# Cached attention beside a small expert: the first key units in other pieces

## The chip, the core and the metric

The kernel runs on one core of a Trainium2 chip. The metric is device time in microseconds. Before the change three runs took 1275.46, 1275.97 and 1275.99 us; the median is 1275.97. The profile shows one further execution of the same program, which took 1275.56 us.

## What is computed

One token passes a layer norm, and then two branches run side by side, whose results are added to it: attention with grouped queries over a long cache, and a one-token expert.

```
xn = layernorm(x)                       # x: 1 x 448
q  = (xn @ wq)                          # 16 query heads of 256
k, v: 8 heads, 65536 positions of 256, bf16; two query heads share one
p  = softmax(q k^T / 16);  o = p v
out = x + o @ wo + xn + sigmoid(xn @ w_r) * ((silu(xn @ w_gate) * (xn @ w_up)) @ w_down)
```

Keys and values are 537 MB of the 549 MB that the kernel reads. All of it is read once and used for a single token.

## The kernel before

The cache is cut into 32 key units and 32 value units of 8,192 KB (four of each per head): 128 partitions with 128 cache rows of 256 elements each, 64 KB in a partition. The SBUF ring has three slots of one unit. Key units use slots 0 and 1 in turn, value units slot 2. The query weights lie in slot 2 before the first value unit does.

A key unit is worked through in 8 sets of 16 rows per partition. For each set TensorE transposes the keys in 16 matmuls (`ps_t`), VectorE and ScalarE copy the result to `kt_all`, and 8 matmuls form the scores (`ps_q`). Four sets are half a unit. A value unit is one block of 64 matmuls (`ps_o`) with the softmax weights `p_sb`.

TensorE's program is a loop over turns, one for each key unit `u` (`turn_K`, line 790). In turns 0 to 3 there are only keys, since the first head's softmax needs the maximum over its four units. From turn 4 on, the value block of unit `u - 4` stands between the first four sets and the last four. In turn 4 the maximum of head 0 is completed on the way through the first four sets, and the exponentials of head 0 stand before the value block.

Two turns make one pass of TensorE's loop, an even and an odd one, so the waits of all even turns share one place in the code. A wait whose count changes from turn to turn compares with a register there.

SP issues all large transfers on one queue, in a fixed order (lines 306 to 331): two pieces of the query weights, key units 0 to 3, value unit 0, key units 4 and 5, and then value unit and key unit in turn. Each issue waits for the slot to be free: `FREE u` is the last transpose of key unit `u`, `FREEH u` the last of its first half, `VFREE t` the end of value block `t`. SP works these waits off one after the other, so a transfer whose wait isn't met holds back all later ones.

`slot_item` (line 277) issues a unit whole or in pieces; each piece has a semaphore of its own. `HALVED` (line 71) names the key units that are loaded in two halves: 0 to 4. For these SP waits with the first half of unit `u` only for `FREEH u - 2`, and TensorE starts on a unit when its first half has landed (`k_sets`, line 770).

Of the kernel before, what the change touches and what calls it, by code (L numbers as in the profile page):

```python
# [12 lines left out]
CH = 64  # L13
# [11 lines left out]
def bass_parallel_sum__gqa_block_cached__moe_arch_mod__decode_kernel(  # L25
# [36 lines left out]
    SETN = NG * GN  # L62
    CSETS = CH // SETN
    SBN = HC * CH
    SETS = SBN // SETN
    U = NPP // SBN
    NT = U * (Hkv - 1)
    NU = U * Hkv
    NTB = NG
    UH = U + 1  # L70
    HALVED = (0, 1, 2, 3, 4)
    assert rep == 2 and NH == 2 and U * SBN == NPP and U % 2 == 0
    assert 2 * D % P == 0 and RP % 2 == 1 and FK % 2 == 0 and Hq % 2 == 0 and FB <= 512
    inv_sqrt_dh = float(Dh) ** -0.5
# [7 lines left out]
    WQN, WGN, WDN, WON = RP * HqDh // 2, RP * F, FH * D, rep * NH * D  # L82
# [17 lines left out]
    wq_area = slots[2][:, 0:WQN]  # L100
# [100 lines left out]
    def SEM(name):  # L201
        s = nc.semaphore("sem_" + name)
        handles.append(s)
        sems[name] = s.__enter__()
        return name

    for n_ in ["pe", "act", "dve", "pool", "qk", "jt", "evq", "exp", "pc", "qc", "sc", "w0", "out", "wq", "wg", "wo", "wd", "we0", "we1", "we2", "wo2", "wo3", "half0", "half1", "res"]:
        SEM(n_)
    for i in range(NTB):
        SEM(f"ev{i}")  # L210
# [21 lines left out]
    def W(e, *key):  # L232
        put(e, "w", key, None, None)
# [3 lines left out]
    def O(e, key, fn, sem=None, n=1):  # L237
        key = key if isinstance(key, tuple) else (key,)
        if not ghost[0]:
            weight[key] = n  # L240
        put(e, "o", key, fn, sem or e)

    def alias(e, *key, sem=None):
        put(e, "a", key, None, sem or e)
# [14 lines left out]
    items = {}  # L259
# [4 lines left out]
    def item(key, parts, need=()):  # L264
        for n in need:
            W("sp", *n)
        for ap, src, sem in parts:
            semtot[sem] = semtot.get(sem, 0) + 16
            items[key] = (sem, semtot[sem])
            prog["sp"].append(("d", here[0], ("DMA", key, len(prog["sp"])), (ap, src), sem))  # L270

    def rows_src(kd, u, o, J):
        src = A_k_cache if kd == "k" else A_v_cache
        n0 = (u % U) * SBN + o
        return src[0, u // U].rearrange("(p n) d -> p n d", p=P)[:, n0:n0 + J, :]

    def slot_item(kd, u, s, parts=None, need=()):

        o = 0
        for k, (sem, J) in enumerate(parts or [("slot%d" % s, SBN)]):  # L280
            ap = slots[s][:, o * Dh:(o + J) * Dh]
            item((kd, u, k), [(ap.rearrange("p (j d) -> p j d", d=Dh), rows_src(kd, u, o, J), sem)],
                 need[k] if isinstance(need, dict) else need if k == 0 else ())
            o += J
        fed[(kd, u)] = (s, parts or [("slot%d" % s, SBN)])

    def flat_src(src, n):
        return src.rearrange("a b -> (a b)").rearrange("(p n) -> p n", p=P)
# [7 lines left out]
    def k_item(u):  # L296
        need = [("FREE", u - 2)] if u >= 2 else ()
        if u >= 2 and u in HALVED:
            need = {0: [("FREEH", u - 2)], 1: need}
        slot_item("k", u, u % 2, [("slot%d" % (u % 2), CH), ("half%d" % (u % 2), CH)] if u in HALVED else None, need)  # L300

    def v_item(t):
        slot_item("v", t, 2, None, [("VFREE", t - 1)] if t else [("QT",), ("R",), ("CONST",)])

    WQ1 = WQN // 4
    item("wq", [(wq_area[:, a:b], flat_src(A_wq, WQN)[:, a:b], "wq") for a, b in ((0, WQ1), (WQ1, WQN))])
    for u in range(U):
        k_item(u)
    v_item(0)
    k_item(U)  # L310
    k_item(U + 1)
    for t in range(1, NT):
        v_item(t)
# [24 lines left out]
    def W_item(e, key):  # L338
        W(e, "DMA", key)
# [98 lines left out]
    pe = nc.tensor  # L438

    def mm(*a, **k):  # L440
        return pe.matmul(*a, **k)  # L441

    def pe_setup():
        W("pe", "XE")
        W("pe", "CONST")

        def xnt(it):
            for c in range(2 * NE):
                ins = mm(ps_m[0:P, C_XNT + c:C_XNT + c + 1],
                         lhsT=xe_row[0:1, :, :, :].rearrange("o b c p -> o (b c) p")[:, c, :],  # L450
                         rhs=sel_bf[0:1, 0, 0:1], start=True, stop=True)
            return ins

        O("pe", "XNT", xnt, n=16 * U)
        W("pe", "XNTSB")
        W_item("pe", "wq")

        def qrow(it):
            for h in range(RP):
                for j in range(NG):  # L460
                    ins = mm(q_rows[32 * j:32 * j + rep, :], lhsT=xnT_sb[:, 2 * h:2 * h + 2], rhs=wq_area[:, (NG * h + j) * QN:(NG * h + j + 1) * QN],
                             start=h == 0, stop=h == RP - 1, tile_position=(0, 32 * j))
            return ins

        W("pe", "PSQ_ZERO")
        O("pe", "QROW", qrow, "jt", 2)
        W("pe", "QROWSB")

        def qt(it):
            half = Hq * NH // 2  # L470
            for f in range(half // NG):
                w = q_row[0:QROWS, f // NH * Dh:(f // NH + 1) * Dh].rearrange("s (x f) -> s x f", f=NH)[:, :, f % NH]
                ins = mm(ps_m[0:P, C_Q:C_Q + 2 * half].rearrange("p (i j f) -> p j i f", i=rep, j=NG)[:, :, :, f], lhsT=w,
                         rhs=sel_bf[0:QROWS, :, :], start=True, stop=True)
            return ins

        O("pe", "QT", qt, "qk", 2)
        W("pe", "PSO_ZERO")
        W("pe", "S2Z")
        W("pe", "KZ")  # L480
        W("pe", "z_q")
# [5 lines left out]
    def k_T(s, m, ap, j):  # L487
        e = ev_engine(m)
        kv = ap.bitcast(FP32).rearrange("p (j d) -> p j d", d=P)
        W("pe", "EV", s - 1, m)  # L490

        def f(it):
            for jj in range(GN):
                ins = mm(ps_tf[m][:, jj * P:(jj + 1) * P], lhsT=kv[:, j + GN * m + jj, :], rhs=ident_f[:, :],
                         is_transpose=True, start=True, stop=True)
            return ins

        O("pe", ("T", s, m), f, f"t{m}")
        kt, tb = kt_buf[(s * NG + m) % NKT], ps_t[m]
        W(e, "T", s, m)  # L500
        if TORD.index(m) < 2:
            W(e, "QK", s - 1)
        if e == "dve":
            O(e, ("EV", s, m), lambda it: nc.vector.tensor_copy(out=kt[:, :], in_=tb[:, :]), f"ev{m}")  # L504
        else:
            O(e, ("EV", s, m), lambda it: nc.scalar.activation(out=kt[:, :], in_=tb[:, :], func=ACTF.Copy), f"ev{m}")  # L506

    def k_QK(s):
        u, sl = divmod(s, SETS)
        x = sl  # L510
        if x == 0:
            W("pe", "EVQ", u - 1)
        if sl == 0:
            W("pe", "QC", u)
        for m in range(NG):
            W("pe", "EV", s, m)

        def f(it):
            for hf in range(NH):
                for m in range(NG):  # L520
                    kt = kt_buf[(s * NG + m) % NKT]
                    ins = mm(ps_q[32 * m:32 * m + SETS * rep, 0:512], lhsT=q_pad[:, hf, (SETS - 1 - x) * rep:(2 * SETS - 1 - x) * rep],
                             rhs=kt[:, :].rearrange("p (k f) -> p f k", f=NH)[:, hf, :],
                             start=(hf == 0 and x == 0), stop=(hf == NH - 1 and x == SETS - 1), tile_position=(0, 32 * m), skip_group_check=True)
            return ins

        O("pe", ("QK", s), f, "qk")
        if x < SETS - 1:
            return
        W("act", "QK", s)  # L530
        W("act", "JT", u - 2)
        O("act", ("EVQ", u), lambda it: nc.scalar.activation(out=s2[u % 2][0:SROWS, :], in_=ps_q[0:SROWS, :], func=ACTF.Copy), "evq")  # L532
        if sl == SETS - 1 and u < NU - 1:
            O("act", ("QC", u + 1), lambda it: nc.scalar.activation(
                out=q_cur[:, :, :], in_=qT_sb[:, :, bass.ds(it * rep + rep, rep) if u + 1 >= U else slice(0, rep)], func=ACTF.Copy), "qc")
# [234 lines left out]
    def k_sets(u, sets, at):  # L770
        ap = slots[u % 2]
        for q in sets:
            if q % CSETS == 0:
                W_item("pe", ("k", u, 0) if q == 0 else ("k", min(u, UH - 1 - (UH - 1 - u) % 2), 1))
            s = u * SETS + q
            for n, m in enumerate(TORD):
                k_T(s, m, ap, q * SETN)
                if n == NG - 1 and (q + 1) % CSETS == 0:
                    alias("pe", "FREE" if q == SETS - 1 else "FREEH", u, sem=f"t{m}")
                if (q, n) in at:  # L780
                    at[(q, n)]()
                if n == 1:
                    k_QK(s - 1)
            k_JT(s - 2)
# [155 lines left out]
    dve_setup()  # L940
    act_setup()
    pe_setup()
    for u in range(NU):
        turn_K(u)
# [274 lines left out]
```

## Time and profile before

| what | value |
|---|---|
| median of three runs | 1275.97 us |
| profiled execution | 1275.56 us |
| its span | 1274.2 us |
| TensorE (PE) busy | 939.5 us, 74% |
| VectorE (DVE) busy | 571.6 us, 45% |
| ScalarE (ACT) busy | 329.3 us, 26% |
| transfers | 549.18 MB, mean 431 GB/s |

The span runs from the first to the last instruction of the profiled execution; what lies around it is 1.4 us. All times in the rows below are microseconds from the start of the span. Busy shares are means over the whole run, in which several stages follow each other. SPq is the sequencer that issues the transfers.

### The profile page before, as it was taken

The numbers are of one execution on the slowest core, as the hardware profiler recorded it, in microseconds if no ns is written. First come the engines' busy times: TensorE is split into PE (matmuls) and PEld (weight loads), VectorE is DVE, ScalarE is ACT, GpSimd is POOL, SyncE is SP. The second block draws the span as 40 slices with busy tenths as digits, with TensorE's granted clock in tenths as the row PEclk, the third lists the DMA queues.
The fourth block names the chain that finished last, engine by engine and source line by source line (L and its number), as shares of the span: only waits on it lengthen the run. The fifth ranks groups of instructions, "written<-read, shape, count | busy, mean of one in ns | idle before, by whom it ended". The sixth has DMA issues, their size and how long they took to land.

```text
span 1274.2 us, 21262 instructions
## 1 busy us (share of the span) xinstructions
PE 939.5 (74%) x8812; PEld 577.8 (45%) x8812; DVE 571.6 (45%) x1086; ACT 329.3 (26%) x432; POOL 9.1 (1%) x38
## 2 busy tenths in 40 slices
PE   4997977678777679777778776687676687766744
PEld 2665544445444445444445444454344454444412
DVE  5775644355344454443454444454444543434410
ACT  1333422132222322222222222222222222222200
POOL 2000000000000000000000000000000000000000
PEclk9998988789888898888898888898888988888885
DMA  9999999999999999999999999999999999999998
GB/s 405 429 435 426 451 430 430 432 432 434 442 430 430 432 432 436 440 430 430 432 432 440 436 432 428 432 432 440 436 432 428 434 430 446 432 430 428 431 437 364
DMA packets 11812, 549.18 MB, mean 431 GB/s; under 512 B 1303, under 2 KB 1690, under 8 KB 2202
## 3 DMA queue, kind: packets, MB, share of 16 engines
q1 hardware_dynamic: 11796, 549.03, 99.7%
q8 instruction: 7, 0.11, 0.0%
q14 instruction: 3, 0.02, 0.0%
q10 hardware_dynamic: 6, 0.00, 0.0%
HBM read 549.03 MB, written 0.00 MB: 431 GB/s over the span
## 4 chain that ended last, share of the span: by engine, by line
DMA 78%; PE 20%; issue 1%; DVE 0%; ACT 0%; SPq 0%; DVEq 0%
DMA ring<-in_A_v_cache_dram 74%; PE ps_o L441 13%; DMA ring<-in_A_k_cache_dram 5%; PE ps_t L441 5%; PE ps_q L441 1%; PE ps_m L441 1%; PE ps_s L441 0%; DVE kt_all L504 0%; ACT S_sb L590 0%; SPq L983 0%; DVE m1p L560 0%; DVE S_sb L558 0%; ACT p_sb L600 0%; DVE kt_all L932 0%; DVE diag L575 0%
## 5 line engine op out<-in xcount | busy, mean ns | idle before, releaser
L441 PE MATMUL ps_t<-ident_f,ring 128*128 128x128 f32 x4096 | 583.8, 288 | 76.8 <-DMA ring<-in_A_k_cache_dram 76.4
L504 DVE COPY kt_all<-ps_t 128x1024 bf16<-128x1024 bf16 x768 | 489.8, 684 | 293.2 <-PE ps_q L441 287.5
L441 PEld LDWEIGHTS ps_t<-ident_f,ring 128*128 128x128 f32 x4096 | 454.2, 144 | 251.5 <-issue 133.8
L506 ACT ACTIVATE kt_all<-ps_t 128x1024 bf16<-128x1024 bf16 x256 | 261.9, 1023 | 490.1 <-PE ps_t L441 489.8
L441 PE MATMUL ps_o<-ring,p_sb 128*4 128x512 bf16 x2048 | 183.1, 522 | 217.8 <-DMA ring<-in_A_v_cache_dram 214.7
L441 PEld LDWEIGHTS ps_o<-ring,p_sb 128*4 128x4 bf16 x2048 | 54.7, 103 | 313.5 <-issue 292.3
L441 PE MATMUL ps_q<-kt_all,q_pad 128*16 128x512 bf16 x2056 | 168.0, 402 | 4.7 <-DVE kt_all L504 1.3
L613 DVE RECIPROCAL rs<-ps_m 128x4 f32<-128x4 f32 x29 | 5.3, 183 | 277.3 <-PE ps_m L441 277.3
L600 ACT ACTIVATE p_sb<-S_sb 128x128 bf16<-128x128 bf16 x64 | 18.9, 307 | 274.7 <-PE ps_o L441 274.4
L648 DVE CAST ob_sb<-ps_o 100x512 bf16<-100x512 f32 x29 | 20.1, 692 | 101.3 <-PE ps_o L441 101.3
L441 PEld LDWEIGHTS ps_q<-kt_all,q_pad 128*16 128x16 bf16 x2056 | 28.8, 86 | 51.7 <-issue 26.7
L532 ACT ACTIVATE s<-ps_q 112x512 bf16<-112x512 f32 x33 | 19.7, 597 | 118.3 <-PE ps_q L441 118.3
L441 PEld LDWEIGHTS ps_m<-rowsum,ones_f 128*128 128x128 f32 x58 | 12.3, 264 | 23.1 <-issue 23.1
L590 ACT ACTIVATE S_sb<-S_sb,negmax 128x512 bf16<-128x512 bf16 x16 | 13.3, 856 | 23.3 <-DVE negmax L584 23.3
L441 PE MATMUL ps_m<-diag,ones_f 2*128 2x2 f32 x58 | 11.1, 258 | 11.2 <-DVE diag L575 11.2
L441 PEld LDWEIGHTS ps_m<-diag,ones_f 2*128 2x128 f32 x58 | 8.6, 184 | 18.1 <-DVE diag L575 18.1
L560 DVE TENSOR_REDUCE m1p<-S_sb (+1 forms) x33 | 13.9, 422 | 4.4
L441 PE MATMUL ps_m<-rowsum,ones_f 128*128 128x4 f32 x58 | 14.9, 326 | 0.0
L558 DVE CAST S_sb<-ps_s 128x256 f32 (+1 forms) x33 | 13.7, 414 | 1.9 <-PE ps_s L441 1.9
L441 PE MATMUL ps_m<-sel_bf,ring 1*128 1x1 bf16 (+1 forms) x12 | 0.6, 168 | 13.6 <-DVE ring L406 12.8
L441 PE MATMUL ps_s<-sel_bf,s 128*128 128x64 bf16 x132 | 9.2, 193 | 0.7 <-ACT s L532 0.7
L532 ACT ACT_TABLE_LOAD x7 | 9.0, 1283 | 1.3 <-issue 1.2
(97 smaller groups left out, 132.4 us busy)
## 6 DMA issues: line engine op xcount, KB each, us to landing
ring<-in_A_k_cache_dram SPq DMA_DIRECT2D x10, 4096.0 KB, 28.6
ring<-in_A_v_cache_dram SPq DMA_DIRECT2D x2, 4096.0 KB, 27.9
ring<-in_A_wq_dram SPq DMA_DIRECT2D x1, 2688.0 KB, 11.1
ring<-in_B_w_gate_dram SPq DMA_DIRECT2D x1, 1568.0 KB, 16.4
ring<-in_B_w_up_dram SPq DMA_DIRECT2D x1, 1568.0 KB, 19.8
ring<-in_B_w_down_dram SPq DMA_DIRECT2D x1, 1568.0 KB
ring<-in_A_wo_dram SPq DMA_DIRECT2D x1, 1344.0 KB, 35.2
ring<-in_A_wo_dram SPq DMA_DIRECT2D x1, 1120.0 KB, 24.9
```

The source lines that it names most:

```text
L441: return pe.matmul(*a, **k)
L504: O(e, ("EV", s, m), lambda it: nc.vector.tensor_copy(out=kt[:, :], in_=tb[:, :]), f"ev{m}")
L506: O(e, ("EV", s, m), lambda it: nc.scalar.activation(out=kt[:, :], in_=tb[:, :], func=ACTF.Copy), f"ev{m}")
L532: O("act", ("EVQ", u), lambda it: nc.scalar.activation(out=s2[u % 2][0:SROWS, :], in_=ps_q[0:SROWS, :], func=ACTF.Copy), "evq")
L558: O("dve", ("SCOPY", u), lambda it: nc.vector.tensor_copy(out=S_sb[:, at(it, SBN), :], in_=ps_sn), "sc")
L560: O("dve", ("SMAX", u), lambda it: nc.vector.tensor_reduce(out=m1p[:, :, at(it, 1)], in_=S_sb[:, at(it, SBN), :].rearrange("p n i -> p i n ...
L590: O("act", ("EXP", h, i), lambda it, i=i: nc.scalar.activation(out=S_sb[:, :, i], in_=S_sb[:, :, i], func=ACTF.Exp, bias=negmax[:, i:i + 1 ...
L600: O("act", ("PC", t, c), lambda it: nc.scalar.activation(out=p_sb[:, c, :, :], in_=S_sb[:, n:n + CH, :], func=ACTF.Copy), "pc")
L613: O("dve", ("RS", t), lambda it: nc.vector.reciprocal(out=rs[:, :, :], in_=ps_m[0:P, C_TOT:C_TOT + NH * rep]))
L648: O("dve", ("OB", t), lambda it: nc.vector.tensor_copy(out=ob_sb[0:OROWS, :], in_=ps_o[0:OROWS, :]))
```

## The change

Units 1, 2 and 4 are loaded whole, with one semaphore. Unit 3 stays in halves. Unit 0 comes in three pieces: a quarter, a quarter and a half, counted by the semaphores `slot0`, `part` and `half0`. The first piece of the query weights counts on `half1` instead of `wq`; unit 1's wait for a second half, which stands at the same place as unit 3's in the odd turns, is met by that count.

```diff
-    UH = U + 1
-    HALVED = (0, 1, 2, 3, 4)
+    HALVED = (3,)
+    FIRST = (CH // 2, CH // 2, CH)
@@ k_item
-        slot_item("k", u, u % 2, [("slot%d" % (u % 2), CH), ("half%d" % (u % 2), CH)] if u in HALVED else None, need)
+        parts = [("slot%d" % (u % 2), CH), ("half%d" % (u % 2), CH)] if u in HALVED else None
+        slot_item("k", u, u % 2, parts if u else list(zip(("slot0", "part", "half0"), FIRST)), need)
@@ query weights
-    item("wq", [(wq_area[:, a:b], flat_src(A_wq, WQN)[:, a:b], "wq") for a, b in ((0, WQ1), (WQ1, WQN))])
+    for k, (a, b, sem) in enumerate(((0, WQ1, "half1"), (WQ1, WQN, "wq"))):
+        item(("wq", k), [(wq_area[:, a:b], flat_src(A_wq, WQN)[:, a:b], sem)])
+    items[("k", 1, 1)] = items[("wq", 0)]
@@ pe_setup
-        W_item("pe", "wq")
+        W_item("pe", ("wq", 0))
+        W_item("pe", ("wq", 1))
@@ k_sets
-            if q % CSETS == 0:
-                W_item("pe", ("k", u, 0) if q == 0 else ("k", min(u, UH - 1 - (UH - 1 - u) % 2), 1))
+            if q == 0:
+                W_item("pe", ("k", u, 0))
+            elif u % 2 == 0 and q * SETN in (FIRST[0], FIRST[0] + FIRST[1]):
+                W_item("pe", ("k", 0, 1 if q * SETN == FIRST[0] else 2))
+            elif u % 2 and q == CSETS:
+                W_item("pe", ("k", min(u, HALVED[-1]), 1))
```

What stands on SP's queue at the start of the program, before the change (a shape of 128x16384 is half a unit, 128x32768 a whole one; `sem_t2` counts transposes, that is `FREE` and `FREEH`; `sem_pe` counts value blocks, `VFREE`):

```order
L983 DMA ring<-in_A_wq_dram 128x3584
L983 DMA ring<-in_A_wq_dram 128x10752
L983 DMA ring<-in_A_k_cache_dram 128x16384 x4
L983 DMA ring<-in_A_k_cache_dram 128x16384 [waits sem_t2] x4
L983 DMA ring<-in_A_v_cache_dram 128x32768 [waits sem_pool,sem_dve,sem_qk]
L983 DMA ring<-in_A_k_cache_dram 128x16384 [waits sem_t2] x2
L983 DMA ring<-in_A_k_cache_dram 128x32768 [waits sem_t2]
L983 DMA ring<-in_A_v_cache_dram 128x32768 [waits sem_pe]
```

The same place on SP's queue after the change:

```order
L991 DMA ring<-in_A_wq_dram 128x3584
L991 DMA ring<-in_A_wq_dram 128x10752
L991 DMA ring<-in_A_k_cache_dram 128x8192 x2
L991 DMA ring<-in_A_k_cache_dram 128x16384
L991 DMA ring<-in_A_k_cache_dram 128x32768
L991 DMA ring<-in_A_k_cache_dram 128x32768 [waits sem_t2]
L991 DMA ring<-in_A_k_cache_dram 128x16384 [waits sem_t2] x2
L991 DMA ring<-in_A_v_cache_dram 128x32768 [waits sem_pool,sem_dve,sem_qk]
L991 DMA ring<-in_A_k_cache_dram 128x32768 [waits sem_t2] x2
L991 DMA ring<-in_A_v_cache_dram 128x32768 [waits sem_pe]
```

Unit 2 is one transfer behind one wait instead of two behind two. Unit 4 is one transfer as well, and stands with unit 5 after value unit 0. The order of the units is what it was.

TensorE, the first two to three sets of an even turn, before (`ps_s` are the transposed scores of the unit before, `sem_ev0` and the like count the copies out of `ps_t`):

```order
L441 MATMUL ps_s<-sel_bf,s_1 128x32x2 [waits sem_sc]
L441 MATMUL ps_s<-sel_bf,s_1 128x32x2 x3
L441 MATMUL ps_t<-ident_f,ring 128x128 [waits sem_ev0]
L441 MATMUL ps_t<-ident_f,ring 128x128 x3
L441 MATMUL ps_t<-ident_f,ring 128x128 [waits sem_ev1]
```

And after:

```order
L444 MATMUL ps_s<-sel_bf,s_1 128x32x2 [waits sem_sc]
L444 MATMUL ps_s<-sel_bf,s_1 128x32x2 x3
L444 MATMUL ps_t<-ident_f,ring 128x128 [waits sem_ev0,sem_part]
L444 MATMUL ps_t<-ident_f,ring 128x128 x3
L444 MATMUL ps_t<-ident_f,ring 128x128 [waits sem_ev1]
```

The third set of an even turn waits for `part`, which only unit 0 raises; from then on the wait is met. No instruction of TensorE's matmuls has moved.

## Rows read from the trace of the kernel before

**Rows 1.** The page's slices, sums of transfers and the large queue.

```profile
DMA  9999999999999999999999999999999999999998
...
DMA packets 11812, 549.18 MB, mean 431 GB/s; under 512 B 1303, under 2 KB 1690, under 8 KB 2202
...
q1 hardware_dynamic: 11796, 549.03, 99.7%
```

**Rows 2.** What SP's queue waited for: us in total, times, longest.

```profile
SPq L983 <- PE ps_o L441: 798.8, 29, 28.7
```

**Rows 3.** Stretches: length, busy us of PE to POOL, granted clock, DMA share, GB/s.

```profile
2.50:20.00 17.50, 3.80 (x40) 1.25 (x40) 10.21 (x24) 2.07 (x4) 5.96 (x20) 1.00 1.03 440
20.00:112.50 92.50, 88.93 (x784) 60.08 (x784) 63.01 (x107) 34.81 (x40) 0.00 (x0) 1.00 1.00 430
112.50:120.00 7.50, 0.00 (x0) 0.00 (x0) 0.75 (x2) 1.68 (x2) 0.00 (x0) 0.68 0.99 425
...
175.00:1180.00 1005.00, 747.37 (x6974) 462.89 (x6976) 451.30 (x858) 261.88 (x341) 0.00 (x0) 0.89 1.00 434
```

**Rows 4.** The chain that ended last: start, us, what.

```profile
0.81 0.39 SPq L983
...
1.26 0.42 SPq L983
...
1.73 20.31 DMA ring<-in_A_k_cache_dram
...
79.63 40.50 DMA ring<-in_A_k_cache_dram
...
140.15 28.39 DMA ring<-in_A_v_cache_dram
...
168.67 3.58 PE ps_o L441 x32
...
174.92 32.32 DMA ring<-in_A_v_cache_dram
```

**Rows 5.** SP's issues in order of time: start, us, what.

```profile
35.02 0.33 SPq L983 DMA_DIRECT2D ring<-in_A_k_cache_dram  x1
...
46.35 0.33 SPq L983 DMA_DIRECT2D ring<-in_A_k_cache_dram  x1
...
68.46 0.33 SPq L983 DMA_DIRECT2D ring<-in_A_k_cache_dram  x1
...
90.39 0.33 SPq L983 DMA_DIRECT2D ring<-in_A_k_cache_dram  x1
...
112.31 0.33 SPq L983 DMA_DIRECT2D ring<-in_A_k_cache_dram  x1
...
150.82 0.33 SPq L983 DMA_DIRECT2D ring<-in_A_k_cache_dram  x1
...
1272.92 0.26 SPq L983 DMA_DIRECT2D out_dram<-kt_all  x1
```

**Rows 6.** PE in order of time; in brackets the idle time before.

```profile
17.68 0.28 PE L441 MATMUL ps_m<-sel_bf,ring 98*128 98x8 bf16 x4 [0.80 <-DVE ring L429]
22.08 1.97 PE L441 MATMUL ps_t<-ident_f,ring 128*128 128x128 f32 x8 [4.13 <-DMA ring<-in_A_k_cache_dram]
...
120.17 1.97 PE L441 MATMUL ps_t<-ident_f,ring 128*128 128x128 f32 x8 [7.89 <-DMA ring<-in_A_k_cache_dram]
```

**Rows 7.** Half-microsecond stretches, columns as in rows 3.

```profile
114.50:115.00 0.50, 0.00 (x0) 0.00 (x0) 0.00 (x0) 0.50 (x1) 0.00 (x0) 1.00 0.46 197
...
125.00:125.50 0.50, 0.50 (x4) 0.50 (x4) 0.47 (x1) 0.20 (x1) 0.00 (x0) 0.50 1.67 721
125.50:126.00 0.50, 0.50 (x6) 0.44 (x4) 0.23 (x1) 0.00 (x0) 0.00 (x0) 1.00 0.61 262
...
173.00:173.50 0.50, 0.50 (x12) 0.23 (x8) 0.00 (x0) 0.00 (x0) 0.00 (x0) 0.71 2.12 918
```

**Rows 8.** Issues by line: size and us from issue to landing.

```profile
ring<-in_A_wq_dram SPq DMA_DIRECT2D x1, 2688.0 KB, 11.1
```

More of the change, by code (lines that the diff above doesn't have):

```diff
@@ L205, in SEM @@
         return name
-    for n_ in ["pe", "act", "dve", "pool", "qk", "jt", "evq", "exp", "pc", "qc", "sc", "w0", "out", "wq", "wg", "wo", "wd", "we0", "we1", "we2", "wo2", "wo3", "half0", "half1", "res"]:
+    for n_ in ["pe", "act", "dve", "pool", "qk", "jt", "evq", "exp", "pc", "qc", "sc", "w0", "out", "wq", "wg", "wo", "wd", "we0", "we1", "we2", "wo2", "wo3", "half0", "half1", "part", "res"]:
         SEM(n_)
```

## The prediction, on record before the changed kernel ran

> **What bounds the kernel now.** I read the page's slices first: the DMA line stands at 9 in every slice but the last, and one queue's packets fill 99.7% of 16 engines' span [rows 1]. By stretches the DMA share is 0.99 to 1.03 from 2.5 us on, while PE is busy 88.93 of 92.50 us in the stretch 20 to 112.5 and idle in 112.5 to 120 [rows 3]. So the transfers set the time, and whatever PE does, all 549 MB have to come through. A transfer is added to the end only where the queue runs dry. For that the reader needs SP's waits: SP issues each transfer when PE has freed the slot, and it waits a total of 798.8 us for PE's value products [rows 2]. Those waits are harmless as long as the next issue comes before the transfer in flight is done.
>
> The pace comes from the chain of waits. Value landings are 140.15 + 28.39 = 168.54 and 174.92 + 32.32 = 207.24 [rows 4]. Between the two lie one key unit and one value unit: 38.70 us, so 19.35 us for a whole unit. Counted back from 168.54, key unit 5 lands at 149.19, unit 4 at 129.84, v0 at 110.5, unit 3 at 91.1, unit 2 at 71.8, unit 1 at 52.4. Counted forward from the first half of unit 0 (1.73 + 20.31 = 22.04) unit 1 would land at 51.1, so these early landings are known to about 1 us.
>
> **Part by part.** *Query weights under two semaphores, register arithmetic in the even turn gone.* PE waits for both pieces before the same product as before; the one ALU instruction was a sequencer step beside 90 us of PE work. I cost both at nothing; the DMA queue, full at that time, hides them.
>
> *Unit 0 in three.* PE begins at 22.08, when the first half has landed; its setup ends at 17.68 + 0.28 = 17.96 [rows 6]. A quarter lands some 4.8 us earlier than a half (a quarter of 19.35), at 17.2, so PE begins at 18.0. The first half of a unit's sets takes 35.02 − 22.08 = 12.94 us after this start [rows 5, 6], to 30.9; the second half of the unit lands at 31.7 to 32.5, PE takes another 46.35 − 35.02 = 11.33 us [rows 5], and frees slot 0 at about 43.2 instead of 46.35. This 3 us lead is worth nothing: PE waits for unit 1 next.
>
> *Unit 1 whole.* Before, PE went on to unit 1's first half without a stop. Now it waits from 43.2 for the whole unit, at about 52: 9 us idle. It then starts with the clock down, as at 22.08, where the whole unit took 46.35 − 22.08 = 24.3 us; the later units take 90.39 − 68.46 = 21.9 and 112.31 − 90.39 = 21.9 [rows 5]. So units 1, 2 and 3 are freed at 76.3, 98.2 and 120.1, 8 us later than before.
>
> Is any transfer late by that? The rule I use: an issue must come 2.5 us before the preceding transfer lands (that value is worked out below). Unit 2: issue 43.2, limit 49.9. Unit 3, first half: 52 + 12.9 = 64.9, limit 69.3. Unit 3, second half: 76.3, limit 81.4 − 2.5 = 78.9, a margin of 2.6. v0, next in SP's order: right behind it. Unit 4, now whole and so issued at 98.2 instead of 79.63 [rows 4]: limit 108. Unit 5: 120.1, limit 127.3. All are in time.
>
> *Unit 4 whole.* This is the term that counts. In the turn of unit 4 PE does half of its key sets, then the first value block, and the end of that block is what SP waits for to issue v1. Before, the first half landed at 79.63 + 40.50 = 120.13 and v1 was issued at 140.15 [rows 4]: 20.02 us. PE could start half a transfer early. Now it waits for the whole unit: 129.84, less what the three undivided units save. That saving is bounded above by the halved stretch: from 22.04 to 120.13 are 98.09 us for five units, 1.34 more than 5 × 19.35, or 0.27 a unit, 0.8 for three; from below it is 0 (unit 0 has one cut more). I take 0.1: landing at 129.7. PE's work from there is the same list of instructions after an idle time of 9.6 us instead of 7.89 [rows 6], so v1 is issued at 129.7 + 20.0 = 149.7. Its limit is 149.1 − 2.5 = 146.6. It is late, the queue runs dry, and nothing later gives the time back.
>
> The clock is a part of these 20 us. It was granted at 1.00 (2.4 GHz) until after PE stopped, was at 0.50 (1.2 GHz) when PE restarted at 120.17, and came back at 125.5, after 5.3 us of work; after the restart at 168.67 it came back between 173.0 and 173.5, after 4.3 to 4.8 us [rows 4, 6, 7]. Both idle times are long enough for it to fall, so I carry the penalty over unchanged and allow 0.7 us either way, the scatter of such returns.
>
> *The price of an empty queue.* The trace shows only one start into an empty queue with a load of many rows: the query weights, issued at 0.81 and 1.26, the second piece landing 11.1 us after its issue, at 12.36 [rows 4, 8]. Both pieces, a quarter and three quarters of 3,584 KB, are 8.47 us at 19.35 us for 8,192 KB, so from the first issue to the landing 3.1 us lie beyond the transfer. From the other side the tiny output transfer, issued at 1272.92, has landed by the end of the span, 1274.2: 1.3 us at most [rows 5]. I take 2.5, nearer to the weights, which are the same kind of load but have shorter rows. Then v1 lands at 149.7 + 2.5 + 19.35 = 171.55, 3.0 us after 168.54. By the ends: 1.8 and 3.6.
>
> The Trainium skill has a price for this too ("DMA: Bandwidth & Descriptors", section "Anatomy of one DMA — SWDGE (gpsimd) path"): a fit of about 2.0 us fixed plus the bytes over 436 GB/s, measured on another issue path than SP's. By it v1 would take 21.2 us, the loss would be 2.4 us and the time 1278.4. For queued transfers the trace disagrees with paying the fixed part each time, since 38.70 us for two units leave 0.1 us apiece over the fit's variable part [rows 4].
>
> *After v1.* Unit 6 is issued 150.82 − 140.15 = 10.7 us after v1 [rows 4, 5], at 160.4, limit 169. v2 needs the block of turn 5: half a unit of sets after 160.4 brings it to about 177.7 (174.92 before [rows 4]), limit 188. The margin of 10 us is back, and the rest of the run is the old one, shifted. *The end* follows the last landing in both.
>
> **Sum.** The profiled execution took 1275.56 us (span 1274.2). 1275.56 + 3.0 = 1278.56. It lies 0.41 under the median of the runs, 1275.97, so on the scale of the median I forecast 1279.0. A difference of 0.2%, about what a measurement of this kernel can tell from no change, is 2.55 us.
>
> **Rivals.**
> 1. *The late issue is hidden or nearly so.* If PE's 20.0 us shrank by 1 us or more (clock back sooner, unit 4 landing 0.8 sooner) and the restart cost the 1.3 of the lower bound, the loss would be 1275.97 + 0 to 1.5: 1276 to 1277.5. For it: the lateness is only 3 us of a path of 150. Against: the same instructions ran after the same kind of idle time, and all these must come together.
> 2. *A second dry spot before unit 3's second half.* Its margin is 2.6 us, on landings known to 1 us. If unit 1 took 4 us longer than I say (its start with the clock down lasting longer), about 1.5 us would be lost there, and unit 4 and v1 would move by as much: 1280.5. Against: 24.3 us already holds one restart.
> 3. *Faster: the early start of PE is paid out.* The chain of waits runs through PE from 22.08 to 79.63, before it goes over to the transfers [rows 4, 6]. Were the keys' work the limit there, beginning at 18.0 would give back 4.1 us: 1271.9. It would need the queue to have run dry in this stretch, and its share is 1.00 at 430 GB/s against 434 later [rows 3]; the difference, 0.9 us in 92.5, is the most that could be won, and only with v1 in time.
>
> **Chances.** A dry queue before v1 with a loss of 1.5 to 4.3 us: 0.76; of this 0.55 lies over 2.55. Rival 1: 0.13. Rival 2: 0.08. Rival 3 or a small gain of whole pieces: 0.03. So faster 0.03, within 0.2% 0.34, slower 0.63. The range: from 3.0 downward 1.2 for the cheap restart, 0.7 for the clock and 0.5 for the landing of unit 4 give 0.6; upward 0.6, 0.7 and a little of rival 2 give 4.6: 1276.6 to 1280.6.
>
> **What would show it.** PE's first key transposes at about 18.0, and a wait of PE for the key transfer of some 9 us ending at about 52, which is new. Unit 3 freed at about 120, PE waiting until 129.7. v1 issued by SP at about 149.7, a dip of the DMA share in the slices of 148 to 151.5, and v1's landing at about 171.5; from there every landing 3.0 later at a spacing of 38.70. I am wrong if the DMA share has no dip there, if there is one before 148, or if the spacing changes.

## The result and the profile after

The changed kernel takes 1279.79 us (median of 7 runs, 1279.04 to 1282.12) against 1275.77 for the kernel before (7 runs, 1275.46 to 1275.99). The ratio is 1.0035 with a 95% interval of 1.0024 to 1.0047: slower by 4.0 us, where 3.0 were forecast. The profiled execution took 1279.79 us, its span is 1278.4, 4.2 more than before.

The page of the changed kernel has the sums that answer to [rows 1]: the same bytes, one more digit 8 in the slices of the DMA line, and a queue that is busy 99.4% of the time instead of 99.7%.

```profile
DMA  9999899999999999999999999999999999999998
...
DMA packets 11524, 549.18 MB, mean 430 GB/s; under 512 B 1271, under 2 KB 1658, under 8 KB 2170
...
q1 hardware_dynamic: 11508, 549.03, 99.4%
```

The stretches of the changed kernel (columns as in [rows 3]) show where it is. Up to 112.5 us PE does less than before (83.13 us busy instead of 88.93), and the transfers go on all the same. From 136 to 175 the DMA share is 0.94, where the kernel before has 1.00. Six hundredths of 39 us are 2.3 us. After 175 the rate is the old one.

```profile
20.00:112.50 92.50, 83.13 (x716) 56.42 (x716) 57.50 (x99) 31.95 (x37) 0.00 (x0) 0.93 1.01 435
...
136.00:175.00 39.00, 36.11 (x392) 22.79 (x394) 24.15 (x49) 14.87 (x22) 0.00 (x0) 1.00 0.94 400
175.00:1180.00 1005.00, 750.68 (x6964) 465.80 (x6960) 451.41 (x857) 261.95 (x341) 0.00 (x0) 0.88 1.00 433
```

In the kernel before, the stretch with the gap and the slice in the middle of it:

```profile
136.00:175.00 39.00, 32.48 (x337) 19.15 (x338) 17.58 (x35) 10.90 (x17) 0.00 (x0) 0.91 1.00 432
...
147.00:149.50 2.50, 2.50 (x32) 1.97 (x28) 1.89 (x3) 1.02 (x1) 0.00 (x0) 1.00 1.03 446
```

In slices of the same columns the gap of the changed kernel has its edges. The view counts a packet where it begins, and between 146.5 and 149.5 no packet with data begins. In the trace's packet records the last ones before the gap end between 146.6 and 148.6, and v1's first ones begin between 149.96 and 150.99.

```profile
146.00:146.50 0.50, 0.50 (x16) 0.18 (x8) 0.00 (x0) 0.00 (x0) 0.00 (x0) 1.00 0.61 262
146.50:147.00 0.50, 0.50 (x10) 0.27 (x2) 0.00 (x0) 0.14 (x1) 0.00 (x0) 1.00 0.01 0
147.00:149.50 2.50, 2.50 (x40) 1.33 (x40) 0.68 (x2) 0.47 (x2) 0.00 (x0) 1.00 0.00 0
149.50:150.00 0.50, 0.50 (x9) 0.33 (x11) 0.19 (x1) 0.00 (x0) 0.00 (x0) 1.00 1.09 393
```

SP's issues in the changed kernel, to be read beside [rows 5] (start, duration): unit 2, the two halves of unit 3, unit 5, and then v1 at 149.00.

```profile
45.37 0.33 SPq L991 DMA_DIRECT2D ring<-in_A_k_cache_dram  x1
...
65.62 0.33 SPq L991 DMA_DIRECT2D ring<-in_A_k_cache_dram  x1
...
76.37 0.33 SPq L991 DMA_DIRECT2D ring<-in_A_k_cache_dram  x1
...
120.24 0.33 SPq L991 DMA_DIRECT2D ring<-in_A_k_cache_dram  x1
...
149.00 0.33 SPq L991 DMA_DIRECT2D ring<-in_A_v_cache_dram  x1
```

PE's restarts in the changed kernel, beside [rows 6] (start, duration; idle time before, in brackets): the first transposes, unit 1 with its new wait, and unit 4.

```profile
20.59 1.94 PE L444 MATMUL ps_t<-ident_f,ring 128*128 128x128 f32 x8 [2.68 <-issue]
...
52.30 1.97 PE L444 MATMUL ps_t<-ident_f,ring 128*128 128x128 f32 x8 [6.96 <-DMA ring<-in_A_k_cache_dram]
...
129.76 1.97 PE L444 MATMUL ps_t<-ident_f,ring 128*128 128x128 f32 x8 [9.55 <-DMA ring<-in_A_k_cache_dram]
```

The issues view of the stretch around 149 gives v1's time from issue to landing; in the kernel before it is 28.4 us there, 9.0 of them until unit 5 has landed (149.19) and 19.35 for v1 itself.

```profile
ring<-in_A_v_cache_dram SPq DMA_DIRECT2D x1, 22.0
```

So v1 lands at 171.0 instead of 168.54, 2.5 us late. The end is 4.2 us late. The chain of waits shows when the difference grows. A value landing late in the run was at 1141.79 + 33.00 = 1174.79 and is now at 1145.00 + 32.43 = 1177.43, 2.64 later; the last value piece was at 1233.90 + 32.37 = 1266.27 and is now at 1237.60 + 32.90 = 1270.50, 4.23 later. First the chain of the kernel before:

```profile
1141.79 33.00 DMA ring<-in_A_v_cache_dram
...
1233.90 32.37 DMA ring<-in_A_v_cache_dram
```

Then that of the changed one. Between the two it has a new piece, a wait for the output weights:

```profile
1145.00 32.43 DMA ring<-in_A_v_cache_dram
...
1184.97 27.38 DMA ring<-in_A_wo_dram
...
1237.60 32.90 DMA ring<-in_A_v_cache_dram
```

The loss therefore has two parts: about 2.6 us from the gap before v1, and about 1.6 us that appear between 1177 and 1270. Landing by landing the trace narrows that down: the one at 1204.32 is 2.65 late, and that of the first output weights, at 1212.35, is 4.22 late. The second part was not forecast.

### The profile page after: what moved, and what is told of

The parts are those of the page before. It is cut to its first block, busy times and chain, and to the rows that moved or that the text cites. A ratio compares the mean times of both kernels' runs of the same rounds, so it can differ in the third digit from the quotient of the medians.

```text
span 1278.4 us, 21261 instructions
## 1 busy us (share of the span) xinstructions
PE 946.4 (74%) x8812; PEld 582.1 (46%) x8812; DVE 571.6 (45%) x1086; ACT 329.3 (26%) x432; POOL 9.1 (1%) x38
## 3 DMA queue, kind: packets, MB, share of 16 engines
q1 hardware_dynamic: 11508, 549.03, 99.4%
## 4 chain that ended last, share of the span: by engine, by line
DMA 77%; PE 21%; issue 1%; DVE 1%; SPq 0%; ACT 0%; DVEq 0%
DMA ring<-in_A_v_cache_dram 68%; PE ps_o L444 13%; DMA ring<-in_A_k_cache_dram 6%; PE ps_t L444 5%; DMA ring<-in_A_wo_dram 2%; PE ps_q L444 2%; PE ps_m L444 1%; DVE kt_all L508 0%; SPq L991 0%; PE ps_s L444 0%; ACT S_sb L594 0%; DVE kt_all L749 0%; DVE m1p L564 0%; DVE ring L895 0%; DVE S_sb L562 0%
## 5 line engine op out<-in xcount | busy, mean ns | idle before, releaser
L444 PE MATMUL ps_q<-kt_all,q_pad 128*16 128x512 bf16 x2056 | 168.5, 403 | 5.8 <-DVE kt_all L508 1.3
L536 ACT ACT_TABLE_LOAD x7 | 9.0, 1283 | 1.3 <-issue 1.2
```

## The experiments

**Which part of the change, and is it the late issue?** Unit 4 alone whole, in the kernel before:

```diff
-    HALVED = (0, 1, 2, 3, 4)
+    HALVED = (0, 1, 2, 3)
-                W_item("pe", ("k", u, 0) if q == 0 else ("k", min(u, UH - 1 - (UH - 1 - u) % 2), 1))
+                W_item("pe", ("k", u, 0) if q == 0 else ("k", min(u, 2 + u % 2), 1))
```

> The kernel before with one part of the change: unit 4 whole, units 0 to 3 in halves as they were. Theory (v1 is issued late because turn 4 starts late): unit 4 lands at 129.8, v1 is issued between 149.0 and 149.9, v1 lands 2.5 to 3.4 us after the 168.54 of before, and the kernel takes 1279 to 1281. Rival (the loss comes from the other parts, PE's new wait for unit 1 above all): within 0.5 us of before, 1275.3 to 1276.3.

It took 1280.51 us (5 runs) against 1275.53 for the kernel before (22 runs beside it); the ratio is 1.0040, interval 1.0027 to 1.0054. The issue of v1 stands at 149.30, and its time to landing is 22.0 us again: it lands at 171.25, 2.7 late. This one part of the change gives the whole loss.

```profile
149.30 0.33 SPq L983 DMA_DIRECT2D ring<-in_A_v_cache_dram  x1
...
ring<-in_A_v_cache_dram SPq DMA_DIRECT2D x1, 22.0
```

Next the dose: unit 4 cut at 96 of its 128 rows, and at 112, with everything else as before. The edit of the first kernel (the second has 112 in the place of 96; `@@` names the function where lines are left out):

```diff
-    HALVED = (0, 1, 2, 3, 4)
+    HALVED = (0, 1, 2, 3)
+    CUT = 96
@@ k_item
+        if u == U:
+            return slot_item("k", u, 0, [("slot0", CUT), ("half0", SBN - CUT)], need)
@@ k_sets
-                W_item("pe", ("k", u, 0) if q == 0 else ("k", min(u, UH - 1 - (UH - 1 - u) % 2), 1))
+                W_item("pe", ("k", u, 0) if q == 0 else ("k", min(u, 2 + u % 2), 1))
+            elif u % 2 == 0 and q * SETN == CUT:
+                W_item("pe", ("k", min(u, U), 1))
```

> The kernel before with unit 4 cut into three quarters and one quarter instead of two halves. Theory: the first piece lands a quarter of a unit later than the first half did, at 125.0, v1 is issued at 144.2 to 145.0, before the limit of about 146.4 (149.1 less 2.7), and the time is that of before, 1275.3 to 1276.3, although PE waits 4.8 us longer. Rival (each microsecond that PE starts later in turn 4 is paid): about half of what unit 4 whole costs, 1277.5 to 1278.

> The kernel before with unit 4 cut into seven eighths and one eighth. Theory: the first piece lands at 127.4, v1 is issued at 146.7 to 147.5, at the limit or up to 1 us past it; v1 lands 0 to 1 us late and the time is 1275.5 to 1278. Rival (a threshold in the pieces' form, whole against cut): 1275.8 with no gap. Rival (linear in PE's delay): 1278.5.

Cut at 96 it took 1276.12 us, ratio 1.0005 (0.9996 to 1.0014): no loss that can be told, although PE's wait before turn 4 is 12.72 us. Cut at 112 it took 1277.68, ratio 1.0016 (1.0007 to 1.0025), where the theory had allowed 1275.5 to 1278. PE's start in turn 4, the issue of v1 and its time to landing, first with the cut at 96:

```profile
124.76 1.97 PE L444 MATMUL ps_t<-ident_f,ring 128*128 128x128 f32 x8 [12.72 <-DMA ring<-in_A_k_cache_dram]
...
144.55 0.33 SPq L988 DMA_DIRECT2D ring<-in_A_v_cache_dram  x1
...
ring<-in_A_v_cache_dram SPq DMA_DIRECT2D x1, 23.8
```

And with the cut at 112:

```profile
147.35 0.33 SPq L988 DMA_DIRECT2D ring<-in_A_v_cache_dram  x1
...
ring<-in_A_v_cache_dram SPq DMA_DIRECT2D x1, 22.1
```

The first is the mark of a transfer that still queues: 23.8 us, and a landing at 168.3, as before. The second found an empty queue: 22.1 us from issue to landing, at 169.4. A delay of PE of half the size (4.6 us, 120.17 to 124.76) costs nothing that can be told, which speaks against a price for every microsecond of it; the limit lies between an issue at 144.6 and one at 147.3.

**The late issue by itself.** In the kernel before, with all units cut as they were, SP's issue of v1 was held back until a later key set of unit 4 had been transposed, the seventh and in a second kernel the eighth (`T` is a set's transposes):

```diff
@@ v_item (the second kernel has + 7 in the place of + 6)
+        more = [("T", U * SETS + 6, TORD[-1])] if t == 1 else []
-        slot_item("v", t, 2, None, [("VFREE", t - 1)] if t else [("QT",), ("R",), ("CONST",)])
+        slot_item("v", t, 2, None, [("VFREE", t - 1)] + more if t else [("QT",), ("R",), ("CONST",)])
```

> The kernel before, all units cut as before, but SP's issue of v1 also waits for the transposes of the seventh key set of unit 4, which end at about 148.1. Nothing else is late. Theory: the queue runs dry, v1 lands at 148.1 + 2.7 + 19.35 = 170.2, 1.6 us late. In the changed kernel the end moved by 4.2 us where v1's landing moved by 2.5; if these further 1.7 us come from the dry queue itself (the 16 engines start level again and one of them later falls behind), the time here is about 1278.5 to 1279.5. If they belong to another part of the change, it is 1277.0 to 1277.6. Rival (an issue that late is still hidden): 1275.8.

> As the run with v1 held back to the seventh set, but held back to the eighth and last key set of unit 4, which ends at about 150.8. Theory (every microsecond past the limit is paid once): issue at 150.8, landing 22.05 later as in the four runs whose queue ran dry, at 172.85, 4.3 us late; the end 1.2 to 2.1 more, so 1281 to 1282. Rival (a dry queue costs a fixed amount): 1278.7 as with the seventh set.

They took 1278.68 us, ratio 1.0030 (1.0017 to 1.0042), and 1281.09, ratio 1.0040 (1.0025 to 1.0055). The rows with the seventh set:

```profile
147.75 0.33 SPq L984 DMA_DIRECT2D ring<-in_A_v_cache_dram  x1
...
ring<-in_A_v_cache_dram SPq DMA_DIRECT2D x1, 22.1
```

And with the eighth:

```profile
150.30 0.33 SPq L984 DMA_DIRECT2D ring<-in_A_v_cache_dram  x1
...
ring<-in_A_v_cache_dram SPq DMA_DIRECT2D x1, 21.9
```

2.55 us more delay, 2.4 us more time by the medians, and 1.9 more by the spans of the profiled executions (1277.6 and 1279.5). The same loss comes about without any whole unit, and past the limit most of each further microsecond is paid. Neither rival, hidden or fixed, holds. With the seventh set v1 lands at 169.80, 1.3 late, and each of the next four landings comes a little later still, until it is 1.8 at 248 us; no other kernel shows this, and the reason stays open.

**The other parts of the change.** The changed kernel, with units 2 and 4 cut at 96:

```diff
+    CUT = 96
@@ k_item
+        if u in (2, U):
+            return slot_item("k", u, 0, [("slot0", CUT), ("half0", SBN - CUT)], need)
@@ k_sets
+            elif u % 2 == 0 and q * SETN == CUT:
+                W_item("pe", ("k", min(u, U), 2 if u == 0 else 1))
```

> The changed kernel with units 2 and 4 cut into three quarters and one quarter; unit 0 stays in three pieces, unit 1 whole, unit 3 in halves, and PE's new wait of some 8 us for unit 1 stays. Theory: v1 is issued at about 144.6, nothing is lost, and the time is that of before with the last quarter cut, 1275.3 to 1276.5. Rival (a part of the 4 us belongs to units 0 and 1 or to the later freeing of slot 0 and 1): 1277 or more.

It took 1276.40 us, ratio 1.0004 (0.9995 to 1.0014). v1 was issued at 144.19 and landed 24.3 us later, at 168.5:

```profile
144.19 0.33 SPq L996 DMA_DIRECT2D ring<-in_A_v_cache_dram  x1
...
ring<-in_A_v_cache_dram SPq DMA_DIRECT2D x1, 24.3
```

Unit 1 whole, unit 0 in three and the moved semaphore cost nothing that can be measured, and win nothing. Unit 2 was cut here and whole in the changed kernel, so its own share was bounded only from the other side, by the run with unit 4 alone, which has the full loss without it; no run has unit 2 alone whole.

**The second part of the loss.** In a table PE's start after its wait for the value unit at about 1175, and for the last value piece, each against the kernel before, where they are at 1174.92 and 1266.41:

| kernel | queue ran dry at v1 | at 1175 | at the end | grown by |
|---|---|---|---|---|
| changed | yes | +2.65 | +4.23 | 1.6 |
| unit 4 whole alone | yes | +2.74 | +4.18 | 1.4 |
| cut at 112 | yes | +0.90 | +2.13 | 1.2 |
| v1 held to the seventh set | yes | +1.78 | +3.37 | 1.6 |
| v1 held to the eighth set | yes | +3.72 | +5.31 | 1.6 |
| cut at 96 | no | −0.24 | +0.57 | 0.8 |
| changed, cut at 96 | no | −0.05 | +0.17 | 0.2 |

It is larger after a dry queue, also where the code of the change is absent. The trace's records of semaphore increments say what differs. A transfer raises its semaphore 16 times, and the profile's page counts 16 DMA engines; I read each increment as one engine's part that has landed, and the landing is the last of them. Before, v1's increments lie 1.96 us apart: eleven within 0.6 us, one at 0.95 and four at 1.55 to 1.96. At 22 us only one engine was behind, by 0.5 us; the four came apart between 22 and 52 us, when four instruction fetches of 16 KB, at 24.47, 34.32, 42.97 and 48.60, took 1.0 to 1.1 us each of one engine. In the changed kernel, after the gap, all 16 lie within 0.93 us, and in the four other kernels whose queue ran dry within 0.83 to 1.01: a dry queue brings the engines closer together.

At 1205.54 there is another such fetch, between the landing at 1204.32, with a spread of 0.99 us, and the one at 1212.35, with 2.56, and from there one engine is alone behind. A further fetch follows at 1235.99, and at the next landing, 1251.08, a second engine is behind (1250.14, the rest by 1249.33). In the kernel before, the fetch at that place, at 1203.55, left the spread at 2.0 us: the end waited for four late engines anyway, and now for five. In each of the seven kernels of the table the growth falls into one step between two landings, and that fetch lies between the two.

The mean of the 16 increments tells how much was lost in all. In the changed kernel it is 3.3 us later than before at v1, and 3.4 later at 1177 and at the last value piece: it hardly grows any more. So 0.8 us of what appears at the end were lost in the gap already, in which the engines that were ahead stood still for longest (v1's first increment is 3.5 late, its last 2.5). The other 0.8 come from one engine being further behind the mean at the end than any was before (1.9 us against 1.1).

The end of the run shows it in the DMA share. The stretches of the kernel before, where the share sinks as one engine after the other finishes, the last ones together:

```profile
1270.00:1271.00 1.00, 1.00 (x48) 0.85 (x38) 0.69 (x1) 0.00 (x0) 0.00 (x0) 0.50 0.53 199
1271.00:1272.00 1.00, 1.00 (x44) 0.78 (x36) 0.16 (x1) 0.00 (x0) 0.00 (x0) 0.50 0.26 89
```

The changed kernel, with about one engine of 16 (0.06) at work in its last two microseconds of transfers:

```profile
1274.00:1275.00 1.00, 1.00 (x48) 1.00 (x44) 0.69 (x1) 0.00 (x0) 0.00 (x0) 0.50 0.23 82
1275.00:1276.00 1.00, 1.00 (x44) 0.73 (x32) 0.16 (x1) 0.00 (x0) 0.00 (x0) 0.50 0.08 27
1276.00:1277.00 1.00, 0.76 (x28) 0.31 (x16) 0.15 (x1) 0.15 (x1) 0.00 (x0) 0.80 0.08 19
```

If that is so, a queue that runs dry after these fetches must not lose anything further. So the kernel before was run with the two last value pieces held back:

```diff
-    slot_item("v", NT + 3, 1, list(zip(LAST_SEMS, LAST)), [("VFREE", NT + 1)])
+    slot_item("v", NT + 3, 1, list(zip(LAST_SEMS, LAST)), [("VFREE", NT + 1), ("PV", NT + 2, 0, 0)])
```

> The kernel before, with the two last value pieces held back until the first half of the value block before them is done, at about 1250.4, where the value unit in flight lands at 1246.8. So the queue runs dry once, but after the instruction fetches of 1203 and 1232. The first piece then lands at 1250.4 + 2.7 + 9.7 = 1262.8 instead of 1256.55, 6.2 us late. Theory (the further 1.2 to 2.1 us at the end of the other runs come from a fetch that falls on engines that a dry queue has set level): no further loss here, last weights 6.2 us late, a profiled time of 1281.7, and the spread of the 16 engines back under 1.2 us. Rival (a dry queue costs that much more at the end wherever it lies): 1283 to 1284.

One execution took 1282.64 us, span 1280.8, which is 6.6 over that of before. SP issued both pieces from 1250.93, half a microsecond later than expected. PE's start on the two, in the kernel before:

```profile
1256.69 3.66 PE L441 MATMUL ps_o<-ring,p_sb 128*4 128x512 bf16 x32 [3.68 <-DMA ring<-in_A_v_cache_dram]
1266.41 3.58 PE L441 MATMUL ps_o<-ring,p_sb 128*4 128x512 bf16 x32 [6.07 <-DMA ring<-in_A_v_cache_dram]
```

And in this one:

```profile
1263.22 3.85 PE L441 MATMUL ps_o<-ring,p_sb 128*4 128x512 bf16 x32 [10.70 <-DMA ring<-in_A_v_cache_dram]
1272.90 3.58 PE L441 MATMUL ps_o<-ring,p_sb 128*4 128x512 bf16 x32 [5.84 <-DMA ring<-in_A_v_cache_dram]
```

They are 6.53 and 6.49 late. The delay does not grow. The increments of the second piece lie within 0.56 us, and the share stays full until all engines stop together:

```profile
1277.00:1278.00 1.00, 1.00 (x48) 0.79 (x40) 0.39 (x2) 0.00 (x0) 0.00 (x0) 0.50 0.99 359
1278.00:1279.00 1.00, 0.98 (x36) 0.51 (x28) 0.01 (x1) 0.00 (x0) 0.00 (x0) 0.83 0.15 50
```

The time itself, one run, lies between the two expectations (1281.7 and 1283 to 1284); 0.5 of the difference to the first is the later issue, and another 0.5 lies outside the span (1.84 us against 1.36 before). It is the rows that decide. That level engines fall behind again is shown. That the instruction fetch is what holds the one engine up is not shown by a run that took a fetch away; it rests on time and size. For it: in the kernel before, one, two, four, five and then six engines are behind at the landings after the fetches at 24.47, 34.32, 48.60, 1203.55 and 1232.45. Against: around 1205 a transfer of another shape (`w_down`) lands in the same interval, though only key and value units land around the other fetches.

## Why the prediction was right, point by point

- *The transfers set the time, and only a dry queue adds to it.* Right within what the medians can tell: 12.7 us of waiting in PE cost nothing with the cut at 96 (1.0005, 0.9996 to 1.0014).
- *Unit 0 in three, a lead of 3 us worth nothing.* Right in its price; the lead was smaller. PE began at 20.59, not at 18.0: there is a stop of 2.68 us before it that the view puts down to issue. What it is the trace doesn't say; in the kernel before it would lie within the wait of 4.13 us [rows 6]. Slot 0 came free at 45.37 instead of 46.35.
- *Unit 1 whole: 9 us idle, then 24.3 us.* The wait was 6.96 us, and unit 1 was freed at 76.37 (76.3 forecast). The clock was down as supposed, at 0.50 until 57.8. (For 22.08 this can't be read in [rows 3]: the clock records begin at 26.5, and the view gives 1.00 where it has none. Eight transposes took 1.97 us there, as at 120.17 [rows 6].) All issues ahead of v1 came in time, and rival 2's second gap didn't appear.
- *Unit 4 lands at 129.7.* The restart is at 129.76.
- *20.0 us from there to v1's issue.* 19.28 with the landing at 129.72, shorter by the whole allowance of 0.7 us. The clock was granted again at 132.9, after 3.1 us instead of 5.3 [rows 7]. With unit 4 alone whole it came back after 4.2 us, and the term was 19.65 (129.65 to 149.30): the less time at 0.50, the shorter the term. The slices of the changed kernel:

```profile
132.00:132.50 0.50, 0.50 (x8) 0.00 (x0) 0.00 (x0) 0.00 (x0) 0.00 (x0) 0.50 2.42 1049
132.50:133.00 0.50, 0.50 (x6) 0.38 (x3) 0.19 (x1) 0.26 (x1) 0.00 (x0) 0.57 0.60 262
133.00:133.50 0.50, 0.50 (x7) 0.50 (x6) 0.50 (x2) 0.50 (x3) 0.00 (x0) 1.00 0.60 262
```

- *2.5 us for an empty queue, between 1.3 and 3.1.* 22.0 − 19.35 = 2.65, and 2.55 to 2.75 in the four other dry runs. The Trainium skill's fit ("DMA: Bandwidth & Descriptors", section "Anatomy of one DMA — SWDGE (gpsimd) path") gives an estimate of 21.2 us for v1. SP's path here takes 21.9 to 22.1, so the measurement stands.
- *v1 lands at 171.55, 3.0 late.* 171.0, 2.5 late, the sum of the two deviations. The dip stands at 146.5 to 149.5 and not at 148 to 151.5, since the view counts packets where they begin.
- *After v1.* Unit 6 was issued at 159.65 and v2 at 175.62 (160.4 and 177.7 forecast), both in time.
- *"from there every landing 3.0 later", the end following.* This step failed. The spacing was 38.70 (171.03, 209.72, 248.42), and the delay stayed at 2.5 to 2.65 us for a thousand microseconds; then, between 1204 and 1212, it grew by 1.6. I had treated a landing as one event; it is the latest of 16, and the gap changed how far each engine is behind. The Trainium skill ("DMA: Bandwidth & Descriptors", section "Why a DMA increments its semaphore by 16 and not by 1") says that the engines of a DMA finish independently and that only the full count means that all has landed; the spread of 1.96 us agrees.
- *The sum.* 3.0 us forecast, 4.0 measured by the medians: 0.5 too much for the gap, 1.6 too little for the end. The range and the sign were right; the likeliest value, 1279.0, was 0.8 us low. That it came so near is in part luck, since the two errors go against each other.
- Rivals 1 and 3 did not come about.

## What to carry to other kernels

Where one queue of transfers is full from beginning to end, an edit is to be judged by one question: does any issue now come after the limit, which is the landing of the transfer in flight less the price of an empty queue (here 2.7 us)? Find the place where the margin was thinnest before the change, since here a delay cost nothing that could be told up to there and most of its length beyond. In this kernel that was the first value unit to be replaced: issued at 140.15 with a limit of 146.4, it had 6 us of margin, and loading the unit ahead of it whole put PE back by 9.6 (120.17 to 129.76).

## What the runs showed that was not expected

A dry queue cost more than the first late landing shows. It brings the 16 engines closer together, and around the later fetches of 16 KB one or two of them fall behind (in the changed kernel 14 within 0.85 us, one at 1.67 and one at 2.60 us at the last value piece), which the end pays: 1.2 to 1.6 us in five kernels. The changed kernel's runs also scatter more, 1279.04 to 1282.12 us against 1275.46 to 1275.99; but the two kernels cut at 96, without a gap, spread over 1.8 and 1.5 us, so the gap is not shown to be the reason. None of the eight kernels beats the kernel before: its DMA share of 0.99 to 1.00 from 20 us on [rows 3] leaves no gap that could be closed.
